# Keeping one operand sum of the wd stage in DRAM between two products

## The chip, the cores and the metric

The kernel runs on one core of one Trainium2 chip. The metric is device time in microseconds of one execution. Five engines work side by side, each with its own queue of instructions: TensorE (PE, its weight loads PEld) multiplies, VectorE (DVE) and ScalarE (ACT) do elementwise work, GpSimd (POOL) does nothing here, SyncE (SP) issues nearly all transfers. They wait for each other only where an instruction needs another's result or a buffer that another still uses.

## The reference, cut to what matters

```python
def _A_ref(x, dft_seq_re, dft_seq_im, dft_hid_re, dft_hid_im):
    a = jnp.einsum("bsd,ed->bse", x, dft_hid_re)
    b = jnp.einsum("bsd,ed->bse", x, dft_hid_im)
    return jnp.einsum("ts,bse->bte", dft_seq_re, a) - jnp.einsum("ts,bse->bte", dft_seq_im, b)
...
def _B_ref(x, w1, b1, w2):
    h = jnp.einsum("bsd,df->bsf", x, w1) + b1
    sp = jnp.log1p(jnp.exp(-jnp.abs(h))) + jnp.where(h > 0, h, jnp.zeros_like(h))
    act = h * jnp.tanh(sp)
    return jnp.einsum("bsf,fd->bsd", act, w2)
...
x = A_x
g = _sigmoid((x * gate_w).sum(-1, keepdims=True))
return g * _A_ref(x, ...) + (1 - g) * _B_ref(x, B_w1, B_b1, B_w2)
```

x has 2048 rows and 640 columns, the hidden width of the second branch is 1728, and everything is float32.

## The kernel before, in words

**Arithmetic.** A float32 matrix product is made of three products of a reduced type: each operand is split into a high part and a low part, and high x high, high x low and low x high are added up in PSUM (mm3, line 100). A split (line 91) is one ScalarE copy for the high part and one VectorE subtraction for the low one. A moving operand is a tile of 128 x 512; its two parts lie in one of nine pairs R (rh, rl), to which four pairs of W are lent later. Stationary blocks of 128 x 128 lie in 26 pairs W (wh, wl).

On top of that stands the scheme of Winograd's form of Strassen: a product of 2 x 2 blocks takes seven block products instead of eight, at the price of sums of operands and results.

**Stages.** The kernel forms u = x times the two sequence matrices (stage "seq", four problems), then y = u times the hidden matrices wd (stage "hid", two problems), then the dense layer with mish (steps in narrow pieces), then the product with w2 (stage "out", two problems). u, y and the activations go through DRAM. In each Winograd problem the moving operand has four blocks per k: a11 and a12 (columns t1), a21 and a22 (columns t2); t1 and t2 are two of the four column groups of 512. A problem has three parts, each a list of steps, one step per product and k:

- first() (line 335): the product with a11, and the column of d that isn't part of the 2 x 2 scheme.
- second() (line 376): the products "22", "21", "s2", "s1". Its sums() (line 381) loads a22, a21, a11 and forms s1 = a21 + a22 and s2 = s1 - a11. s2, the fourth product counting first()'s, is split and multiplied, and its tile goes back to the free list.
- third() (line 487): the products "12", "s3", "s4". Its sums() (line 491) loads a12, a11, a21, a22 and forms s3 = a11 - a21, then a22 - s3, which is s2 again, then s4 = a12 - s2. s4 is the operand of the last product.

In the stage of wd there are five k (kh = KD = 5), so second() has 20 steps and third() 15 per problem; in_turn (line 320) gives their order. The two problems follow each other: first() of both, then second() and third() of the first, then of the second.

**Order of the work.** Nothing is ordered by the hardware alone: a planner in the kernel's text, the loop from line 1203, writes out each engine's queue step by step. At step i it issues loads of operands for steps up to LEAD + AHEAD = 7 + 9 ahead, as long as the free list FS of 22 tiles of 128 x 512 keeps a few in reserve (spare, line 1197); it writes the preparation (sums and splits, "preps") of the step 7 ahead; then step i's matmuls; then the stores that are due; then post work and side jobs. A store is registered by store() (line 128) with a lag in steps, and its tile goes back to FS when the store has been issued. A load may not be issued before its source's store has been: `unwritten` holds the tiles that are still to be stored.

**Side jobs** are the preparation of stationary operands, for the current and the coming stages (low and top, quad_job line 644, w1_job line 661, w1c, w1r), and the gating of y. The planner keeps an account, clock["dve"], of the time that it has given to VectorE, and starts or goes on with a job only while that account is below clock["pe"] plus a limit: SLACK = -1 in the stage of wd, SLACK_D = +1 in most of the dense stage. Each tt() (line 84) adds 0.14 + 0.54 x columns/512 to it. A job also needs free tiles of W, FX (four of 128 x 640) and FS. In a few steps around the start of the dense stage ("quiet") no job runs.

The lines that the change touches or the prediction speaks of: the account at line 85, the split at 91 and 250, the matmul at 98, the loads at 147, 152 and 1214, the stores at 1223.

Of the kernel before, what the change touches and what calls it, by code (L numbers as in the profile page):

```python
# [7 lines left out]
F32 = mybir.dt.float32  # L8
F32R = mybir.dt.float32r
AF = mybir.ActivationFunctionType  # L10
OP = mybir.AluOpType

S, D, F = 2048, 640, 1728
P = 128
N = 512
# [12 lines left out]
SLACK, SLACK_UP, SLACK_D, QUIET = -1.0, 2.5, 1.0, 2  # L28
NR, NFS, NFX, NW, NL = 9, 22, 4, 26, 4
MM = 0.2267  # L30
BACK, NB = 16, 3
NLOAD = 6
QUIET_M, D_END = -1, 24
# [21 lines left out]
def fnet_mish_gate(ctx: ExitStack, tc: tile.TileContext, xn, xt, c_re, c_im, wd_re, wd_im,  # L55
# [4 lines left out]
    dr = ctx.enter_context(tc.tile_pool(name="dr", bufs=1, space=bass.MemoryType.DRAM))  # L60
# [4 lines left out]
    FS = Slots([sb.tile([P, N], F32, name=f"f{i}") for i in range(NFS)])  # L65
# [18 lines left out]
    def tt(o, a, b, op):  # L84
        clock["dve"] += 0.14 + 0.54 * a.shape[-1] / N
        nc.vector.tensor_tensor(o, a, b, op=op)  # L86
# [41 lines left out]
    def store(dst, v, f, lag=3):  # L128
        stores.append((dst, v, f, clock["step"] + (lag if clock["step"] < len(steps) - 8 else 0)))
# [117 lines left out]
                                2 + (k % KD == 0) + ((st.kind, k) not in tops), 1, 1))  # L247
            tops.add((st.kind, k))

    def c_split(key, f):  # L250
        r = OPS[key] = R.get()
        split(r[0], r[1], f)
        FS.put(f)

    def op_done(key):
        R.put(OPS.pop(key))
# [63 lines left out]
    def in_turn(kh, begin, between, end):  # L320
# [2 lines left out]
        order += [(p, k) for k in range(2, kh - 2) for p in between]  # L323
        return order + [(p, k) for p in end for k in (kh - 2, kh - 1)]

    class Problem:


        def __init__(self, st, tp, moving, finish, end=False, aside=None):
            self.st, self.moving, self.finish, self.end, self.aside = st, moving, finish, end, aside  # L330
            self.t1, self.t2 = 2 * tp, 2 * tp + 1
            self.out, self.early = st.kind == "out" and not tp, st.kind == "out" and tp


        def first(self, new=False, ks=None):
# [40 lines left out]
        def second(self):  # L376
            st, kh, t1, t2 = self.st, self.st.kh, self.t1, self.t2
            n = len(steps)
            own = {}
# [64 lines left out]
            for p, k in in_turn(kh, ("22", "21", "s2", "s1"), ("22", "21", "s2", "s1"), ("22", "21", "s2", "s1")):  # L444
                i, key = len(steps), ("c", st.kind, len(steps))
                raw, preps = [], []
                if p == "22":
                    raw = [(("a", a, i), self.moving(t, kk)) for a, t, kk in
                           ((22, t2, k + kh), (21, t2, k), (11, t1, k))]
                    preps.append(lambda k=k, raw=raw: (need((st.kind, "low", k)), sums(k, raw)))  # L450

                def mms(p=p, k=k, key=key):
                    for name, b in uses[p](k):
                        product(name, b, key, k == 0 and (p, name) in opens and not (st.kind == "out" and name != "b"),
                                k == kh - 1)
                    op_done(key)
                    if self.end and (p, k) in ends:
                        W.put(st.XA[k])
                        if k == kh - 1:
                            W.put(*[w for w in st.XT2 if w])  # L460
                preps.append(lambda p=p, k=k, key=key: c_split(key, own.pop((p, k))))
                step(raw, preps, mms, lambda p=p, k=k: post(p, k))
                if k == kh - 1:
                    takes[i] = (p == "21" or p == "s1" and 2) if self.early else 1 if p == "21" else 2
                    if self.early and p != "s1":
                        takes[i - 4] = 2
                        if p == "21":
                            self.y_load(i - 4, t2, 4)
                        else:
                            self.y_load(i - 4, *{"22": (t2, 0, 1), "s2": (t1, 2, 3)}[p])  # L470
                if (p, k) == ("21", kh - 1):
                    done = i
# [14 lines left out]
        def third(self, over=False):  # L487
            st, kh, t1, t2 = self.st, self.st.kh, self.t1, self.t2
            own = {}

            def sums(k, raws):
                a12, a11, a21, a22 = (RAW.pop(r[0]) for r in raws)
                tt(a11, a11, a21, OP.subtract)
                FS.put(a21)
                tt(a22, a22, a11, OP.subtract)
                tt(a22, a12, a22, OP.subtract)
                own.update({("12", k): a12, ("s3", k): a11, ("s4", k): a22})

            uses = {
                "12": lambda k: [("c", blocks(st.XB[k], P, 2)), ("d1", blocks(st.XB[k], 0, 1))],  # L500
                "s3": lambda k: [("a", blocks(st.XT13[k], 2 * P, 2))],
                "s4": lambda k: [("b", blocks(st.XB[k], 3 * P, 2))],
            }

            def b_out():
                f, g, (p0, p1) = FS.get(), FS.get(), PS["b"]
                copy(f, p0)
                self.finish(2, t1, f)
                copy(g, p1)
                nc.scalar.dma_start(out[3 * P:4 * P, t1 * N:(t1 + 1) * N], g)  # L510

            def post(p, k):
                if k < kh - 1:
                    return
                if self.early and p == "s4":
                    b_out()
                elif p == "s3":
                    fs = KEEP.pop("p4") + KEEP.pop("p5")
                    for ps, o in zip(PS["a"] * 2, fs):
                        tt(o, ps, o, OP.add)  # L520
                    free_banks("a")
                    for d, o in enumerate(fs):
                        if self.out:
                            at(clock["step"] + d // 2 + 1, lambda d=d, o=o: self.give(d, t2, o))
                        else:
                            self.give(d, t2, o)
                elif p == "12":
                    self.done("c", 0, t1)
                    self.done("d1", 4, t1)
                else:  # L530
                    self.done("b", 2, t1)

            for p, k in in_turn(kh, ("12", "s3", "s4"), ("12", "s3", "s4"), ("s3", "12", "s4")):
                i, key = len(steps), ("c", st.kind, len(steps))
                if self.early and p == "s4" and k >= kh - 2:
                    key = p, k
                raw, preps = [], []
                if (p, k) in {("12", k) for k in range(kh - 2)} | {("s3", kh - 2), ("s3", kh - 1)}:
                    raw = [(("a", a, i), self.moving(t, kk)) for a, t, kk in
                           ((12, t1, k + kh), (11, t1, k), (21, t2, k), (22, t2, k + kh))]  # L540
                    preps.append(lambda k=k, raw=raw: sums(k, raw))

                def by_bank(k=k):
                    j = k - (kh - 2)
                    for kk in (kh - 2, kh - 1):
                        mm3(PS["b"][j], *uses["s4"](kk)[0][1][j], *OPS["s4", kk], False, kk == kh - 1)

                def mms(p=p, k=k, key=key):
                    if self.early and p == "s4" and k >= kh - 2:
                        return by_bank(k)  # L550
                    for name, b in uses[p](k):
                        product(name, b, key, False, k == kh - 1)
                    op_done(key)
                    if self.end and p == "s4":
                        W.put(st.XB[k], st.XT13[k])
                preps.append(lambda p=p, k=k, key=key: c_split(key, own.pop((p, k))))
                step(raw, preps, mms, lambda p=p, k=k: post(p, k))
                if k == kh - 1 and p != "s3":
                    takes[i] = 3 if p == "12" else 2
                if self.out and k == kh - 1:  # L560
                    self.y_load(i - (4 if p == "s3" else 2), *{"s3": (t2, 0, 1, 2, 3), "12": (t1, 0, 1, 4), "s4": (t1, 2, 3)}[p])
                    if p == "s4":
                        at(i, lambda: FS.put(QT.pop(t1), QT.pop(t2)))
                if st.kind == "out" and (p, k) == ("s4", 1):
                    rest(t1, [("c", 0, False), ("c", 1, False), ("d1", 4, False), ("b", 2, False), ("b", 3, False)])
# [481 lines left out]
    unwritten = {id(d) for row in usc + asc + qout for d in row} | {id(d) for d in XD.values()}  # L1047
# [64 lines left out]
    hid = Stage("hid", KD, lambda k: (wd_re, wd_im)[k // KD][k % KD], neg=True)  # L1112
# [7 lines left out]
    hd = [Problem(hid, tp, lambda t, k: usc[k][t], put_y, tp == 1, aside("ph") if tp else None) for tp in range(2)]  # L1120
    ou = [Problem(fin, tp, lambda t, k: asc[k][t], put_out, False, aside("po") if tp else None) for tp in range(2)]

    stage_jobs(seq, [("low", k) for k in range(KH)])
    for k in range(KS):
        jobs.append(Job(("gate", k), simple(lambda f, k=k: gate_rows(k, f)), lambda k=k: [x_rows(k)], fx=1 + (not k)))
# [172 lines left out]
```

## Time and profile before

| what | value |
|---|---|
| median of 3 runs | 861.6 us (861.38 to 861.71) |
| the profiled execution | 862.33 us |
| its span, first to last instruction | 860.5 us |
| matmuls | 3766 |
| read from HBM, written | 180.13 MB, 52.18 MB |

| stretch of the profiled span | what runs |
|---|---|
| 0 to 397 us | stage seq |
| 397 to 519 us | stage of wd |
| 519 to 687 us | dense stage |
| 687 to 857 us | stage of w2 |

The bounds of the stages come from counting the matmuls of each stage in the code. In a row of the profile's groups "L86 DVE TENSOR_TENSOR f<-f,f ... x50 | 34.5, 689 | 1.0" means line 86 of the kernel, VectorE, output tile and inputs, 50 instructions, 34.5 us busy, 689 ns each, 1.0 us idle before them. A row of a timeline begins with the start and the duration in us. A row of stretches gives, after the stretch and its length, the busy us and the number of instructions of PE, PEld, DVE, ACT and POOL, then the granted clock, the DMA engines' mean share and GB/s. Rows of waits give the engine that waited, for whom, us in total, times and the longest. Rows of transfers give their number, KB each and the median us from issue to landing.

### The profile page before, as it was taken

How to read it: one execution, taken by the hardware profiler on the slowest of the kernel's cores; microseconds unless marked ns; L12 is line 12 of the kernel's file. 1: busy time of each engine (PE TensorE's matmuls, PEld its weight loads, DVE VectorE, ACT ScalarE, POOL GpSimd, SP SyncE). 2: the span in 40 equal slices, each digit the busy share in tenths (PEclk: the TensorE clock that was granted, in tenths of full speed). 3: DMA queues.
4: the chain of work that ended last, by engine and by line, in shares of the span. 5: the costliest groups of instructions: out<-in, count | busy, mean ns of one | idle time of the engine just before them, and what ended most of it. 6: DMA issues, size and time to landing. Idle time of an engine off the chain costs nothing.

```text
span 860.5 us, 12305 instructions
## 1 busy us (share of the span) xinstructions
PE 856.2 (100%) x3766; PEld 708.4 (82%) x3766; DVE 732.6 (85%) x1281; ACT 485.6 (56%) x903; POOL 0.2 (0%) x4
## 2 busy tenths in 40 slices
PE   9999999999999999999999999999999999999998
PEld 8888888888888888888888888888888888888886
DVE  6999988889879789998998897886578979898993
ACT  6756646464555545657656657764646756542442
POOL 0000000000000000000000000000000000000000
PEclk9999999999999999999999999999999999999999
DMA  9975758885768899898676968879998789485952
GB/s 348 345 255 198 252 164 309 281 287 198 255 234 287 280 343 363 274 316 287 207 261 242 319 197 309 287 231 370 357 377 308 230 283 315 152 289 178 353 185 110
DMA packets 126978, 233.15 MB, mean 271 GB/s; under 512 B 14656, under 2 KB 17216, under 8 KB 126912
## 3 DMA queue, kind: packets, MB, share of 16 engines
q1 hardware_dynamic: 126480, 231.72, 77.9%
q8 instruction: 29, 0.48, 0.2%
q10 hardware_dynamic: 432, 0.66, 0.2%
q14 instruction: 37, 0.30, 0.1%
HBM read 180.13 MB, written 52.18 MB: 270 GB/s over the span
## 4 chain that ended last, share of the span: by engine, by line
PE 100%; ACT 0%; issue 0%
PE ps L98 100%; ACT f L89 0%
## 5 line engine op out<-in xcount | busy, mean ns | idle before, releaser
L98 PE MATMUL ps<-rh,wh 128*128 128x512 f32 (+1 forms) x1062 | 412.1, 389 | 0.0
L98 PE MATMUL ps<-rh,wl 128*128 128x512 f32 x1046 | 405.9, 389 | 0.0
L98 PE MATMUL ps<-rl,wh 128*128 128x512 f32 x1045 | 405.9, 389 | 0.0
L89 ACT ACTIVATE rh<-f 128x512 fp32r<-128x512 f32 x419 | 250.8, 626 | 182.7 <-DVE f L86 101.7
L86 DVE TENSOR_TENSOR rl<-f,rh 128x512 fp32r<-128x512 f32 x417 | 272.5, 686 | 41.3 <-ACT rh L89 40.1
L98 PEld LDWEIGHTS ps<-rh,wh 128*128 128x128 f32 x1062 | 199.5, 188 | 41.6 <-DVE f L86 0.3
L98 PEld LDWEIGHTS ps<-rl,wh 128*128 128x128 f32 x1045 | 196.6, 188 | 40.9
L98 PEld LDWEIGHTS ps<-rh,wl 128*128 128x128 f32 x1046 | 196.3, 188 | 40.7
L86 DVE TENSOR_TENSOR f<-f,f 128x512 f32<-128x512 f32 x305 | 208.4, 688 | 9.6 <-DMA f<-act 2.2
L89 ACT ACTIVATE f<-ps 128x512 f32<-128x512 f32 (+1 forms) x145 | 83.2, 596 | 75.2 <-PE ps L98 66.7
L89 ACT ACTIVATE wh<-f 128x512 fp32r<-128x512 f32 (+3 forms) x173 | 76.7, 484 | 46.7 <-DVE f L86 36.5
L86 DVE TENSOR_TENSOR wl<-f,wh 128x512 fp32r<-128x512 f32 (+3 forms) x172 | 82.3, 512 | 20.5 <-ACT wh L89 20.4
L86 DVE TENSOR_TENSOR f<-ps,f 128x512 f32<-128x512 f32 x100 | 65.5, 683 | 16.9 <-PE ps L98 16.7
L98 PE MATMUL ps<-wh,wh 128*128 128x512 f32 x205 | 79.8, 389 | 0.0
L98 PE MATMUL ps<-wl,wh 128*128 128x512 f32 x200 | 77.8, 389 | 0.0
L98 PE MATMUL ps<-wh,wl 128*128 128x512 f32 x199 | 77.4, 389 | 0.0
L98 PEld LDWEIGHTS ps<-wh,wh 128*128 128x128 f32 x205 | 38.5, 188 | 8.2 <-ACT f L89 0.2
L98 PEld LDWEIGHTS ps<-wl,wh 128*128 128x128 f32 x200 | 37.5, 188 | 7.8
L98 PEld LDWEIGHTS ps<-wh,wl 128*128 128x128 f32 x199 | 37.4, 188 | 7.7
L732 ACT ACTIVATE f<-f,b1s 128x512 f32<-128x512 f32 x36 | 25.5, 721 | 31.5 <-DVE f L86 31.5
L86 DVE TENSOR_TENSOR wl<-fx,wh 128x640 fp32r<-128x640 f32 (+3 forms) x50 | 33.7, 680 | 5.9 <-ACT wh L89 5.9
L89 ACT ACTIVATE wh<-fx 128x640 fp32r<-128x640 f32 (+4 forms) x51 | 31.1, 615 | 5.9 <-DMA fx<-in_xn_dram 3.5
(36 smaller groups left out, 176.5 us busy)
## 6 DMA issues: line engine op xcount, KB each, us to landing
f<-in_c_re_dram SPq DMA_DIRECT2D x128, 256.0 KB, 4.0
f<-in_c_im_dram SPq DMA_DIRECT2D x128, 256.0 KB, 4.5
f<-act SPq DMA_DIRECT2D x87, 256.0 KB, 4.9
f<-u SPq DMA_DIRECT2D x80, 256.0 KB, 5.0
act<-f SPq DMA_DIRECT2D x54, 256.0 KB, 5.1
f<-in_xt_dram SPq DMA_DIRECT2D x49, 256.0 KB, 4.6
u<-f SPq DMA_DIRECT2D x40, 256.0 KB, 3.1
y<-f SPq DMA_DIRECT2D x40, 256.0 KB, 4.9
```

The lines of the kernel that those rows point to most:

```text
L86: nc.vector.tensor_tensor(o, a, b, op=op)
L89: nc.scalar.activation(o, a, AF.Copy, scale=scale)
L98: nc.tensor.matmul(ps, a, b, start=start, stop=stop, skip_group_check=True)
L732: nc.scalar.activation(o[rows], src[rows], AF.Mish, bias=b1s[rows, f:f + 1])
```

## The change

Each problem of the stage of wd (S2_OF names "hid" alone) gets five tiles in DRAM, s2[k]. When the s2 of a k has been split in second(), its tile isn't given back at once but stored there, with a lag of one step (S2_LAG). third()'s sums() loads s2[k] in the place of a22 and leaves out the subtraction that forms it again. The new tiles are added to `unwritten`. The other stages stay as they are.

```diff
+S2_LAG, S2_OF = 1, ("hid",)
...
-    def c_split(key, f):
+    def c_split(key, f, dst=None):
         r = OPS[key] = R.get()
         split(r[0], r[1], f)
-        FS.put(f)
+        if dst is None:
+            FS.put(f)
+        else:
+            store(dst, f, f, S2_LAG)
...
+            n = len(problems)
+            problems.append(self)
+            self.s2 = [dr.tile([P, N], F32, name=f"s2_{n}_{k}") for k in range(st.kh)] if st.kind in S2_OF else []
...
-                preps.append(lambda p=p, k=k, key=key: c_split(key, own.pop((p, k))))
+                preps.append(lambda p=p, k=k, key=key: c_split(key, own.pop((p, k)), self.s2[k] if p == "s2" and self.s2 else None))
...
-                tt(a22, a22, a11, OP.subtract)
+                if not self.s2:
+                    tt(a22, a22, a11, OP.subtract)
                 tt(a22, a12, a22, OP.subtract)
...
+                    if self.s2:
+                        raw[-1] = ("s2", i), self.s2[k]
                     preps.append(lambda k=k, raw=raw: sums(k, raw))
...
+    unwritten.update(id(d) for p in problems for d in p.s2)
```

More of the change, by code (lines that the diff above doesn't have):

```diff
@@ L324, in in_turn @@
         return order + [(p, k) for p in end for k in (kh - 2, kh - 1)]
+    problems = []
     class Problem:
```

## The prediction

> **What bounds the kernel now.** I begin with the shares of the engines and the chain that ended last, because a change that takes work from VectorE pays only where VectorE, or something that waits for it, sets the end.
>
> ```profile
> span 860.5 us, 12305 instructions
> ...
> PE 856.2 (100%) x3766; PEld 708.4 (82%) x3766; DVE 732.6 (85%) x1281; ACT 485.6 (56%) x903; POOL 0.2 (0%) x4
> ```
> ```profile
> 0.77 856.26 PE ps L98 x3766
> 857.03 0.02 issue
> 857.05 0.60 ACT f L89
> ```
>
> Of the page's rows the second gives TensorE's matmul track 100% and VectorE 85%. The other three are the chain in order of time: from 0.77 us on, 856.26 us are one unbroken piece of matmuls, and only the last copy and store of the output stand behind it. VectorE is not in the chain.
>
> A busy matmul track could still run slowly, so I look at its rate, by stretches of 100 us, and then at all the waits of TensorE and of its weight loads.
>
> ```profile
> 100.00:200.00 100.00, 100.00 (x443) 82.79 (x442) 89.10 (x151) 49.49 (x84) 0.00 (x0) 1.00 0.77 260
> ...
> 400.00:500.00 100.00, 100.00 (x443) 82.81 (x442) 91.22 (x160) 65.34 (x124) 0.00 (x0) 1.00 0.77 267
> 500.00:600.00 100.00, 100.00 (x442) 82.47 (x441) 81.99 (x161) 64.66 (x134) 0.00 (x0) 1.00 0.80 278
> ```
> ```profile
> PE ps L98 <- PEq L1286: 0.8, 1, 0.8
> ```
> ```profile
> PEld ps L98 <- issue: 0.7, 1, 0.7
> PEld ps L98 <- DVE f L86: 0.3, 1, 0.3
> PEld ps L98 <- ACT f L89: 0.2, 1, 0.2
> ```
>
> 442 or 443 matmuls start in each stretch, whatever VectorE does in it (82 to 91 us of the 100), at a granted clock of 1.00: one about every 0.227 us. TensorE waits once, for 0.8 us, before its first matmul. The weight loads wait three times, 0.7 us at the start and 0.3 and 0.2 us later; those last two are all that the other engines cost TensorE in the whole execution. So there is hardly any waiting that a lighter VectorE could give back.
>
> The Trainium skill, "Perfetto Trace Analysis", section "Identifying the Most-Contended Engine", holds that the busy share of matmuls is no good measure of the distance to the roofline and that the weight loads' share is a better one. By that rule the 82% of the weight loads would say that 18% of the time is headroom. The row of counts decides here: the rate is the same in every stretch, so whatever headroom there is lies inside a matmul's own 0.227 us, and this change leaves number and shape of the matmuls alone.
>
> **The stage of wd.** Each of its two problems has 270 matmuls (45 in first(), 120 in second(), 105 in third()), and the matmuls before it end at 397 us. Behind it stands the dense stage.
>
> ```profile
> 397.00:519.00 122.00, 122.00 (x540) 101.03 (x539) 111.44 (x196) 79.48 (x151) 0.00 (x0) 1.00 0.75 259
> 519.00:580.00 61.00, 61.00 (x270) 50.17 (x269) 49.52 (x105) 43.60 (x94) 0.00 (x0) 1.00 0.78 268
> ```
> ```profile
> L86 DVE TENSOR_TENSOR f<-f,f 128x512 f32<-128x512 f32 x50 | 34.5, 689 | 1.0
> ```
>
> In the stage's 122 us VectorE is busy for 111.4. Of that, 50 sums of two operands take 34.5 us; 50 is what the code makes it, two per k in second() and three in third(), five k, two problems.
>
> **What is removed.** One sum per k in third(): 10 instructions of 689 ns, 6.9 us of VectorE. It comes off an engine that TensorE does not wait for in these 122 us: 0 us of the time. The next rows show how far ahead VectorE's results are; the first writes the low part of an operand, the second is the first matmul that streams it.
>
> ```profile
> 441.31 0.68 DVE L86 TENSOR_TENSOR wl<-f,wh 128x512 fp32r<-128x512 f32 x1
> ```
> ```profile
> 447.04 0.39 PE L98 MATMUL ps<-wl,wh 128*128 128x512 f32 x1
> ```
>
> Ready at 441.99, used at 447.04: 5.0 us of lead, the shortest between 430 and 460 us when I pair all operands with their matmuls in this way. The lead may grow by up to 3.4 us per problem. That has no value by itself.
>
> **What is added.** Ten stores of 256 KB, and ten loads of s2 in the place of ten loads of u, so the number of loads stays.
>
> ```profile
> f<-u SPq DMA_DIRECT2D x80, 256.0 KB, 5.0
> act<-f SPq DMA_DIRECT2D x54, 256.0 KB, 5.1
> ...
> u<-f SPq DMA_DIRECT2D x40, 256.0 KB, 3.1
> ```
> ```profile
> L1223 SPq DMA_DIRECT2D u<-f x40: 319/382/1286, 94.3 to 401.8; - x40
> ```
>
> - Issue: 10 x 382 ns = 3.8 us of SyncE's queue over 122 us. Hidden: loads are issued up to LEAD + AHEAD = 16 steps before their step, and a step here is 225 / 35 = 6.4 matmuls, 1.46 us.
> - Traffic: 2.6 MB more in a stage that moves 259 GB/s, about 10 us at its mean rate or 0.083 of its volume; the engines' share rises from 0.75 to some 0.81. Hidden while the loads keep their lead.
> - The store's own wait: it needs the sum, which VectorE formed before it split 22, 21 and s2 of that k. On SyncE the store comes one step after the split of s2 was planned. At most it waits about 1 us, and the loads of u and of weights queued behind it have some 20 us of lead.
> - The reload's wait for its store to land. Counting out the planner's loops, there are at least six steps between the two for every k, 6 x 1.46 = 8.8 us (some 6 us where SyncE runs in bursts), against a landing after 3.1 (u) to 5.1 us (act). No wait, or a small one.
> - A slot of FS is held for one to three steps longer, and its next load waits for the store's reading instead of for the split. There are 22; the planner then takes a load one or two steps later, out of 16.
>
> No row of before shows this reload. From above it is bounded by store and load in sequence for each k, 10 x (3.1 + 5.0) = 81 us if nothing hid any of it; from below by zero, or by the 0.5 us of the weight loads' later waits if the lighter VectorE removed them. I take zero, because loads of u with the same size, queue and lead delay no matmul.
>
> The Trainium skill, "DMA: Bandwidth & Descriptors", section "Anatomy of one DMA — SWDGE (gpsimd) path", puts most of a fixed 2 us into the receipt of the write, worst for HBM, and its section "Two DMAs through the same engine are not ordered" asks for a wait on the first transfer before a reader is issued. By its fit an estimate for 256 KB is 2.6 us each way; the trace's 3.1 and 5.0 us are longer, and the sum stays zero by both as long as the six steps stand between.
>
> **What is moved.** The planner counts each sum as 0.14 + 0.54 = 0.68 us of VectorE and starts side work when that account is 1 us behind TensorE's. Five sums fewer lower it by 3.4 us per problem, so it draws forward what comes next: the weights of the dense stage.
>
> ```profile
> 449.34 0.90 SPq L147 DMA_DIRECT2D fx<-in_w1a_dram  x2
> ...
> 469.01 1.65 SPq L147 DMA_DIRECT2D fx<-in_w1a_dram  x2
> ...
> 482.25 0.81 SPq L147 DMA_DIRECT2D fx<-in_w1a_dram  x2
> ...
> 511.20 0.80 SPq L147 DMA_DIRECT2D fx<-in_w1a_dram  x2
> ...
> 532.75 3.28 SPq L147 DMA_DIRECT2D fx<-in_w1a_dram  x2
> ```
>
> The pair at 449.34 is issued when the job before it has given its rows back. In the new account that job can start some ten steps sooner, so this load should come at 436 to 442 us. Jobs that need three free pairs of W stay where third() frees them; later, from 511 us on, about one job of w1 (some 4 us of VectorE) gets done before the dense stage instead of in it. In that stage the cover is thin:
>
> ```profile
> 562.42 0.69 DVE L86 TENSOR_TENSOR rl<-f,rh 128x512 fp32r<-128x512 f32 x1
> ...
> 563.60 0.39 PE L98 MATMUL ps<-rl,wh 128*128 128x512 f32 x1
> ```
> ```profile
> 573.21 0.43 DVE L86 TENSOR_TENSOR f<-fx,f 128x256 f32<-128x256 f32 x1
> ...
> 573.55 0.68 DVE L86 TENSOR_TENSOR f<-ps,f 128x512 f32<-128x512 f32 x1
> ...
> 574.29 0.19 PEld L98 LDWEIGHTS ps<-rh,wh 128*128 128x128 f32 x1 [0.30 <-DVE f L86]
> ```
>
> Ready at 563.11, used at 563.60: 0.49 us. And at 574.29 the weight load waited for an add that reads a bank of PSUM and stood behind the preparation of weights; the wait of 0.30 us is the row seen above. If the jobs come earlier, such places get better by up to the 0.5 us; if another piece falls in front of such an add, they get worse.
>
> **Sum**, against the profiled execution: 862.33 = span 860.5 + 1.83 around it. Sums removed 0, stores and loads 0, moved work between -0.5 and some tenths, I take -0.1. That execution lies 0.7 above the median of the runs, 861.6; taken off the median, the forecast is **861.5 us**.
>
> **Rivals.**
> - *A new stall in the dense stage; slower.* The same weights, in another order, can put a burst in front of an add for which TensorE waits. One burst is four sums of 0.42 us (the row at 573.21 is the last of one), 1.7 us, and there are three pairs of fp: 1.7 us if it strikes once, 863.2, and 5.1 if in each, 866.6. It decides from the point where VectorE is more than 0.49 us later than now at such a place. For it: the 0.49 and the 0.30 us. Against it: VectorE is busy for 49.5 of 61 us there and gets less to do, and the planner holds its account to the same limit. From about 590 us on the planner's account of before runs at its floor (3 us behind TensorE), so both schedules meet again.
> - *The reload takes the place of the sum; slower.* If store and load follow each other closely, SyncE stands 5 us for each k, and everything behind it too. It decides when the delay exceeds the lead of the loads, some 20 us: four waits in a row. One problem's five would then cost 5 x 5 - 20 = 5 us, 866.6. Against it: six steps lie between.
> - *VectorE's time counts after all; faster.* All 6.9 us off: 854.7. Against it: the counts by stretches and the list of waits. Half of it would already be past the bound.
> - *The change doesn't do what it says.* If u were still read beside s2, ten more loads would show; the diff replaces the entry in the list, so nothing of this is left but a count to check.
>
> **How the numbers follow.** About 0.2% (1.7 us) is what a measurement of this kernel can tell from no change. The forecast's own case, 861.0 to 862.5, has 0.85; the stall in the dense stage 0.10, the reload 0.02, VectorE's gain 0.03. Within 0.2% thus 0.85, slower 0.12, faster 0.03. The range goes from 861.0 (both later waits gone, and the runs' own spread of 0.3 us below) to 863.2 (one burst).
>
> **What would show it.** Right: TensorE's matmuls again one piece of about 856 us, 3766 of them; f<-f,f in the stage 40 instead of 50, VectorE some 7 us less busy in all; u read 70 times, ten stores to s2 and ten loads; the first weight load after w1b near 440 us instead of 449.34. Wrong: a wait of TensorE or its weight loads of over 0.5 us between 519 and 580 us (first rival), SyncE waiting for s2 to land with operands late behind it (second), fewer than 850 us of matmuls (third).

## The result and the profile after

The changed kernel takes 862.89 us (median of 22 runs, 862.69 to 863.96), the kernel before 861.77 us (22 runs, 861.38 to 862.62). The ratio is 1.0013, 95% interval 1.0007 to 1.0019: slower by 1.1 us. The time is inside the forecast range and within the 0.2%, but its sign is the wrong one: the forecast took 0.1 us off the kernel before, and the interval of the ratio lies wholly on the slower side.

What was to be seen of the change itself is there. These are rows of the page of the changed kernel, one of its groups in the stretch from 397 to 519 us, and three of its transfers (the program's name of the new tiles, numbers left out, is s). All lines have moved down: 87 is the old 86, 90 the old 89, 99 the old 98.

```profile
span 860.9 us, 12296 instructions
...
PE 855.9 (99%) x3766; PEld 707.5 (82%) x3766; DVE 725.4 (84%) x1271; ACT 485.8 (56%) x903; POOL 0.2 (0%) x4
```
```profile
L87 DVE TENSOR_TENSOR f<-f,f 128x512 f32<-128x512 f32 x40 | 26.6, 686 | 0.3
```
```profile
f<-u SPq DMA_DIRECT2D x70, 256.0 KB, 4.8
...
s<-f SPq DMA_DIRECT2D x10, 256.0 KB, 5.4
f<-s SPq DMA_DIRECT2D x10, 256.0 KB, 5.0
```

Ten sums fewer, 7.2 us of VectorE less over the whole execution (732.6 to 725.4), ten loads of u replaced, ten stores added. The time did not come from there. Next the two stretches, and all waits of the weight loads:

```profile
397.00:519.00 122.00, 122.00 (x540) 101.03 (x539) 106.95 (x194) 80.10 (x156) 0.00 (x0) 1.00 0.80 278
519.00:580.00 61.00, 60.37 (x265) 49.14 (x264) 48.50 (x101) 43.34 (x93) 0.00 (x0) 1.00 0.85 293
```
```profile
PEld ps L99 <- ACT f L90: 0.9, 1, 0.9
PEld ps L99 <- DVE f L87: 0.8, 2, 0.6
PEld ps L99 <- issue: 0.7, 1, 0.7
PEld ps L99 <- ACT wh L90: 0.2, 1, 0.2
```

In the stage of wd 540 matmuls start, as before: nothing lost, nothing won. In the 61 us behind it 265 start instead of 270. The waits of 0.2 and 0.3 us of before have grown to 0.9 and 0.8.

To add them up I took the starts of all matmuls from the 21st on, and counted what an interval above 0.229 us exceeds 0.2267 us by. Before: 0.22 us in all, 0.05 us of it around 560 us and 0.17 us from 574 us on. After: 1.37 us, at the same two places, 0.76 us around 559 us (the expectations below write 0.75) and 0.61 us from 573.9 us on. The 1.15 us between the sums is the 1.1 us of the runs. The profiled spans differ by 0.4 us only (860.5 and 860.9), because the first 20 matmuls took 6.77 us in the one profile and 5.89 us in the other. That start differs from profile to profile, though all eleven kernels profiled here begin alike. When it is taken off each span together with the waits, 853.55 to 853.86 us are left in all eleven: start and waits account for the spans to 0.3 us.

The chain that ended last was one piece of matmuls before. Now it breaks in the dense stage (start, us, what):

```profile
0.77 557.77 PE ps L99 x2454
558.54 0.06 issue
558.60 0.02 ACTq L90
558.61 0.13 issue
558.74 0.40 ACT wh L90
559.14 1.46 ACT f L90 x3
...
573.75 0.61 DVE f L87
574.36 0.04 issue
574.40 282.90 PE ps L99 x1246
```

From 558.5 to 574.4 us it runs through ScalarE and VectorE, and behind 574.4 all is matmuls again. So this is the prediction's first rival, in the stretch that it named, and with the sign that it gave for it, a wait of over 0.5 us between 519 and 580 us.

### The profile page after: what moved, and what is told of

The parts are those of the page before. It is cut to its first block, busy times and chain, and to the rows that moved or that the text cites. A ratio compares the mean times of both kernels' runs of the same rounds, so it can differ in the third digit from the quotient of the medians.

```text
span 860.9 us, 12296 instructions
## 1 busy us (share of the span) xinstructions
PE 855.9 (99%) x3766; PEld 707.5 (82%) x3766; DVE 725.4 (84%) x1271; ACT 485.8 (56%) x903; POOL 0.2 (0%) x4
## 4 chain that ended last, share of the span: by engine, by line
PE 98%; DVE 1%; ACT 1%; issue 0%; DVEq 0%; ACTq 0%
PE ps L99 98%; DVE f L87 0%; DVE wl L87 0%; ACT wh L90 0%; ACT f L90 0%; ACT f L744 0%; DVE fx L87 0%; DVE rl L87 0%; ACT rh L90 0%; DVEq L87 0%; ACTq L90 0%
## 5 line engine op out<-in xcount | busy, mean ns | idle before, releaser
L87 DVE TENSOR_TENSOR f<-f,f 128x512 f32<-128x512 f32 x295 | 200.5, 688 | 9.7 <-DMA f<-act 2.7
```

## The experiments

Theory 1: with ten sums fewer in its account the planner starts the side jobs of the dense stage in other steps, and this new order makes TensorE wait. Its rival: the ten stores and reloads, with their traffic and the tiles that they hold, delay something. A third possibility is that VectorE's time in the stage of wd matters in itself. Counted out from the planner's loops, the jobs w1 1 to w1 5 begin at steps 340, 349, 352, 357 and 362 before, and at 329, 340, 349, 354 and 358 in the changed kernel; the steps of the stage end at 335. Counted in the same way, all pieces of all jobs keep the steps of before in the first, the third and the fourth experiment, and those of the changed kernel in the second. All ratios are to the kernel before on the same chip.

### The change in the old order

```diff
                 if not self.s2:
                     tt(a22, a22, a11, OP.subtract)
+                else:
+                    clock["dve"] += 0.14 + 0.54
```

> The change as it is, but the planner's account still adds the 0.68 us of each sum that is left out, so the side jobs run in the order of before. Theory 1 (the new order of the weight jobs in the dense stage is what costs): the time of before, 861.8 us (ratio 0.999 to 1.001), and TensorE's waits between 519 and 580 us back from 1.37 to at most 0.4 us. Rival (the ten stores and reloads cost): the time of the change, 862.9 us, ratio 1.0013, with the waits of over 1 us still there. That VectorE's 6.9 us count: 855 us.

Measured: 861.79 us against 862.17, ratio 0.9997 (0.9988 to 1.0006); TensorE's waits 0.25 us. Sums gone, stores and reloads there, and the time is that of before. The stores and reloads cost nothing that can be seen, and the order of the jobs is all that is left.

### The old arithmetic in the new order

```diff
                 tt(a22, a22, a11, OP.subtract)
+                if st.kind == "hid":
+                    clock["dve"] -= 0.14 + 0.54
```

> The kernel before, its sum formed twice as ever and nothing stored, but the account does not count the ten sums, so the side jobs run in the order of the changed kernel. Theory 1: slower as the change is, 862.9 us or a little more, since VectorE still has the ten sums to do (ratio 1.0008 to 1.003), with waits of 1 to 2.5 us between 519 and 580 us. Rival (stores and reloads cost): 861.8 us, waits 0.2 to 0.4 us.

Measured: 863.43 us against 862.17, ratio 1.0013 (1.0004 to 1.0022), the ratio of the change; waits 1.38 us.

```profile
PEld ps L98 <- ACT f L89: 0.9, 1, 0.9
PEld ps L98 <- DVE f L86: 0.8, 2, 0.6
PEld ps L98 <- issue: 0.7, 1, 0.7
PEld ps L98 <- ACT wh L89: 0.5, 1, 0.5
```

The two rows that count are those of the changed kernel to the tenth. Nothing is stored here and no sum is saved: the new order alone makes the loss.

### The stores alone

```diff
-                if not self.s2:
-                    tt(a22, a22, a11, OP.subtract)
+                tt(a22, a22, a11, OP.subtract)
...
-                    if self.s2:
-                        raw[-1] = ("s2", i), self.s2[k]
```

> s2 is stored as in the change, but third() loads u and forms the sum again; the stored copy is not read. Order of the side jobs as before. Theory 1: 861.8 us (0.999 to 1.001), waits at most 0.4 us. Rival (the stores, their traffic and the tiles held longer cost): some or all of the 1.1 us, 862.3 to 862.9 us.

Measured: 861.88 us against 862.17, ratio 0.9998 (0.9989 to 1.0007); waits 0.23 us. No cost.

### One more sum

```diff
                 tt(a22, a22, a11, OP.subtract)
+                if st.kind == "hid":
+                    nc.vector.tensor_tensor(a21, a12, a22, op=OP.subtract)
                 tt(a22, a12, a22, OP.subtract)
```

a21 goes back to the free list behind these lines instead of ahead of them.

> The kernel before with one more sum for each k in third() of the stage of wd, into a tile that is no longer needed, and not counted in the account: 10 x 0.69 = 6.9 us more of VectorE, the order of everything else as before. Theory 1 with the prediction's first step (VectorE's time in this stage lies beside the matmuls): 861.8 us, 0.999 to 1.001. Rival (VectorE's time in this stage reaches the end, and the dense stage starts later on VectorE): up to 6.9 us more, 868.7, or 0.5 to 2 us if only the rest of it is carried into the dense stage.

Measured: 861.87 us against 862.17, ratio 0.9997 (0.9988 to 1.0006); waits 0.27 us.

```profile
397.00:519.00 122.00, 122.00 (x540) 101.02 (x539) 115.78 (x202) 77.56 (x147) 0.00 (x0) 1.00 0.75 253
```

VectorE is busy for 115.8 of the 122 us, 4.3 more than before in this stretch (and 1.7 more in the next 61 us), and 540 matmuls start as ever. Ten sums of 0.69 us are worth nothing here, added or taken away.

### Where the order bites: one step more before the splits

The first wait in the changed kernel, by its timeline (start, us, engine, what; the bracket gives idle time and what ended it), between the three adds that free banks and the matmul that waits:

```profile
553.72 1.87 DVE L87 TENSOR_TENSOR f<-ps,f 128x512 f32<-128x512 f32 x3
555.51 0.41 DVE L87 TENSOR_TENSOR wl<-fx,wh 128x256 fp32r<-128x256 f32 x1
555.85 0.48 DVE L87 TENSOR_TENSOR wl<-f,wh 128x128 fp32r<-128x128 f32 x2
556.25 0.55 DVE L87 TENSOR_TENSOR wl<-fx,wh 128x384 fp32r<-128x384 f32 x1
556.72 0.41 DVE L87 TENSOR_TENSOR fx<-fx,fx 128x256 f32<-128x256 f32 x1
```
```profile
557.96 0.42 DVE L87 TENSOR_TENSOR f<-fx,f 128x256 f32<-128x256 f32 x1
...
558.42 0.42 ACT L90 ACTIVATE wh<-f 128x256 fp32r<-128x256 f32 x1 [0.61 <-DVE f L87]
...
558.74 0.40 ACT L90 ACTIVATE wh<-fx 128x256 fp32r<-128x256 f32 x1
...
559.05 1.55 ACT L90 ACTIVATE f<-ps 128x512 f32<-128x512 f32 x3
...
559.68 0.19 PEld L99 LDWEIGHTS ps<-wh,wh 128*128 128x128 f32 x1 [0.90 <-ACT f L90]
```

Read it backwards. The weight load at 559.68 waits for the first of three copies out of PSUM (559.05). That copy stands in ScalarE's queue behind two splits of a w1 job (558.42, 558.74), and the first of these waited 0.61 us for the last of the job's four sums on VectorE (557.96). Ahead of the sums VectorE has the last piece of one job (555.51, 555.85) and the first piece of the next (556.25) in a row. In the kernel before, only a first piece stands there:

```profile
554.59 1.87 DVE L86 TENSOR_TENSOR f<-ps,f 128x512 f32<-128x512 f32 x3
556.39 0.54 DVE L86 TENSOR_TENSOR wl<-fx,wh 128x384 fp32r<-128x384 f32 x1
556.86 0.41 DVE L86 TENSOR_TENSOR fx<-fx,fx 128x256 f32<-128x256 f32 x1
```
```profile
559.19 1.57 ACT L89 ACTIVATE f<-ps 128x512 f32<-128x512 f32 x3
```

From the end of the adds to the copy: 559.19 - 556.46 = 2.7 us before, 559.05 - 555.59 = 3.5 us after. The 0.7 us between them are the extra piece (555.51 to 556.25), and nearly all of the wait of 0.76 us. In all of this VectorE's total did not grow: it is busy for 48.5 us of this stretch instead of 49.5.

If that is so, the copy need not wait for any less work, only for its place in the queue to be free (theory 1a). To test it, each w1 job rests two steps instead of one between its sums and its splits:

```diff
         tt(t[:, B2], ga[:, B2], t[:, A2], OP.subtract)
-        yield 1
+        yield 2
```

> The changed kernel, but each w1 job rests two steps instead of one between its four sums and the splits that read them. Theory 1a (ScalarE's queue stands at a split that needs a sum just formed, and the copy that frees a bank stands behind it): the waits of TensorE between 519 and 580 us fall from 1.37 to at most 0.5 us, time 861.8. Theory 1b (VectorE simply has too much to do there): the same work in nearly the same place, waits of 1 us or more, 862.9.

Measured: 862.14 us against 861.91, ratio 0.9999 (0.9991 to 1.0008); waits 0.11 us, less than the kernel before has. ScalarE's queue at the same place:

```profile
557.78 2.05 ACT L90 ACTIVATE f<-ps 128x512 f32<-128x512 f32 x4
559.68 0.44 ACT L90 ACTIVATE wh<-f 128x256 fp32r<-128x256 f32 x1
```

Four copies, the three among them, now run through ahead of the split. But the longer rest also moves the jobs' steps, w1 2 begins at 349 again, and the double piece is no longer there. So this run supports theory 1a and does not tell it from the double piece; the last experiment does.

The Trainium skill, "Perfetto Trace Analysis", section "Optimization Strategy", says that a gap that repeats on the engine that should be saturated can mean too little SBUF or PSUM. The waits here are waits for PSUM banks, and by that rule one would look for more PSUM; with the eight banks that the kernel has, another order of the queues took the waits from 1.37 to 0.11 us.

### The old order and the longer rest

The edits of the first experiment and of this one together.

> The order of before (the ten sums left out but still counted), and the rest of two steps as well. Theory 1a: the waits of before, 0.22 us, go too; 861.6 us, at most 0.3 us below the kernel before, ratio 0.9995 to 1.0. Theory 1b: 861.8 us, waits 0.2 to 0.4.

Measured: 861.97 us against 861.91, ratio 1.0001 (0.9992 to 1.0010); waits 0.10 us. The waits of before are halved, and 0.1 us can't be seen in the time. Nothing more is left to win here: all the waits of the kernel before were worth 0.2 us.

### The double piece split up

```diff
-elif loaded and loaded[0][2] + (5 if i in narrow else 3) <= i and len(W.free) >= loaded[0][0].w:
+elif loaded and i != nm - 1 and loaded[0][2] + (5 if i in narrow else 3) <= i and len(W.free) >= loaded[0][0].w:
```

> The changed kernel, but in the one step where the last piece of a w1 job and the first piece of the next are written in a row (the first step after the pause in which no job runs), the next job starts a step later. All other jobs start as in the changed kernel. Theory 1 in detail (that double piece is what comes in front of the copy that frees the bank at 558.8 us): the first wait falls from 0.75 to at most 0.3 us, the second near 574 us stays at 0.3 to 0.6; time 862.1 to 862.5. If the double piece has no part in it, both stay and the time is 862.9.

Measured: 863.65 us against 861.91, ratio 1.0018 (1.0009 to 1.0026). The first wait is gone, as expected. The second is 1.41 us instead of 0.3 to 0.6, and the sum 1.70 us: a miss in the total.

```profile
554.43 1.87 DVE L87 TENSOR_TENSOR f<-ps,f 128x512 f32<-128x512 f32 x3
```
```profile
574.24 0.56 DVE L87 TENSOR_TENSOR wl<-fx,wh 128x384 fp32r<-128x384 f32 x1 [1.21 <-ACT wh L90]
...
574.72 0.68 DVE L87 TENSOR_TENSOR f<-ps,f 128x512 f32<-128x512 f32 x1
...
575.45 0.19 PEld L99 LDWEIGHTS ps<-rh,wh 128*128 128x128 f32 x1 [1.67 <-DVE f L87]
```

Here the roles are exchanged: the add that frees the bank (574.72) stands on VectorE behind a low part (574.24) that waited 1.21 us for ScalarE. In the changed kernel the add at this place is this one:

```profile
573.66 0.68 DVE L87 TENSOR_TENSOR f<-ps,f 128x512 f32<-128x512 f32 x1
```

The two traces can't be laid on each other by the clock, since their first 20 matmuls differ by 0.7 us (5.89 and 6.61); so I count from the three adds, at 553.72 in the changed kernel and at 554.43 here. The later add follows after 19.94 us there and after 20.29 us here: VectorE comes to it 0.35 us later. TensorE, which no longer lost its 0.76 us at the first place, comes to it that much sooner. Together these are the 1.1 us by which the second wait grew (0.61 to 1.70 us, with what follows it). My expectation took the two waits as separate; what TensorE doesn't lose at the first place it loses at the second, because VectorE is late there all the same.

By the planner's loops all four pieces of the shifted job move by a step, its sums and splits too, and no other job moves. So this run takes away the double piece and gives the copies more room at once, and doesn't show the part of the double piece alone.

### A lower limit in the dense stage

```diff
-SLACK, SLACK_UP, SLACK_D, QUIET = -1.0, 2.5, 1.0, 2
+SLACK, SLACK_UP, SLACK_D, QUIET = -1.0, 2.5, 0.0, 2
```

> The changed kernel with the limit of the account in the dense stage at 0 instead of +1 us. The jobs up to the first wait keep their steps, those after it come later by up to a step. Theory 1: the first wait stays at 0.75 us, the second changes. If the waits hang on VectorE's total in the stage alone: both change together.

Measured in a single run: 863.15 us; waits 0.82 us, the first at 0.77, as in the changed kernel, and the second down to 0.05. One run can't place the time within some tenths, so the trace has to tell. Between 519 and 580 us VectorE is busy for 49.1 us, no less than the 48.5 of the changed kernel. Each wait goes with the steps of the jobs just ahead of it, and not with VectorE's load in the stage.

### One job alone rests longer

```diff
         tt(t[:, B2], ga[:, B2], t[:, A2], OP.subtract)
-        yield 1
+        yield 2 if f == 3 else 1
```

> The changed kernel, with the rest of two steps between sums and splits for one w1 job alone, the one whose splits stand ahead of the first late copy. The double piece ahead of its sums stays where it is, and all jobs begin in the steps of the changed kernel; only this job's last two pieces are written a step later. Theory 1a (the place of the copy in ScalarE's queue): the first wait falls from 0.75 to at most 0.1 us though the double piece is still there. If the double piece itself is what delays the copy: 0.75 stays. The second wait, near 574 us, may grow to as much as 1.4, as it did when a job was shifted by a step; the time would then be 862.5 to 863.5 us.

Measured: 862.60 us against 862.15, ratio 1.0004 (0.9995 to 1.0013), so the time doesn't settle it; the trace does. The waits are 0.66 us, all of them from 574 us on; the first wait is gone.

```profile
556.75 0.48 DVE L87 TENSOR_TENSOR wl<-f,wh 128x128 fp32r<-128x128 f32 x2
557.15 0.55 DVE L87 TENSOR_TENSOR wl<-fx,wh 128x384 fp32r<-128x384 f32 x1
```
```profile
558.12 2.05 ACT L90 ACTIVATE f<-ps 128x512 f32<-128x512 f32 x4
560.03 0.45 ACT L90 ACTIVATE wh<-f 128x256 fp32r<-128x256 f32 x1
```

The double piece is there, last of one job and first of the next, and the copies run through ahead of the split all the same. So both have a part in the first wait: the double piece delays the sum, and the split that waits for it holds the copy. Without the split in front of the copy the wait is gone (this run). With the split in front, but without the extra piece, it is 0.05 us: that is the kernel before, where at this place a first piece, the sums and the splits of a job stand in the same three steps, 349 to 351. The second wait grew less than I allowed for, from 0.61 to 0.66 us: counted from the three adds, VectorE comes to its add 0.68 us sooner than in the changed kernel (573.88 - 554.62 = 19.26 us), nearly as much as TensorE does. Why it comes sooner here and later in the run of the double piece wasn't taken apart any further.

### All runs beside each other

| kernel | waits in the trace, us | median less that of before on the same chip, us |
|---|---|---|
| before | 0.22 | |
| changed | 1.37 | 1.12 |
| change, old order | 0.25 | -0.38 |
| old arithmetic, new order | 1.38 | 1.26 |
| stores alone | 0.23 | -0.29 |
| one more sum | 0.27 | -0.30 |
| longer rest | 0.11 | 0.23 |
| old order, longer rest | 0.10 | 0.06 |
| double piece split up | 1.70 | 1.74 |
| lower limit (one run) | 0.82 | 1.24 |
| one job rests longer | 0.66 | 0.45 |

## Why the prediction was right and where it was wrong

- **What bounds the kernel**: right. In all eleven kernels the time follows TensorE's own waits, within the half microsecond or so that the medians scatter, and the profiled spans follow them to 0.3 us once the first 20 matmuls are taken off. The rate was not quite the same in every stretch, though: the first 100 us hold 428 matmuls, since the first 20 are slower.
- **Sums removed, 0 us**: right, by the run that adds ten more and by the first experiment.
- **Stores and reloads, 0 us**: right, by the first and the third experiment. Two readings in it were off, without effect. The landing took 5.4 us, above the 3.1 to 5.1 that I bounded it by, and between store and reload the planner's loops put five to eight steps, not at least six. No reload had to wait for its store all the same; the closest was issued 1.06 us after its store had landed. SyncE did wait for the stores to land, three times, 4.3 us in all, the longest 2.1 us (the row of its waits reads "SPq L1228 <- DMA s<-f: 4.3, 3, 2.1"). But the run that stores and never reloads has these waits too, 5.0 us in four. The two long ones in the changed kernel, 2.1 and 1.9 us, end at loads of u (434.46 and 489.81) into the very tile that the store was reading: the tile that is held longer, and not the reload. The lead of the loads covered them.
- **What is moved: the step that failed.** That the jobs come earlier was right, and nearly so by how much: the first pair of weights came at 434.9 us instead of 449.3 (forecast 436 to 442), and w1 one job earlier. But the sum's term was "between -0.5 and some tenths, I take -0.1", with the reason that "if the jobs come earlier, such places get better". It measured +1.15 us in the waits and +1.12 us in the time. An earlier job is not a better place: what mattered was which pieces stood in a row between the freeing of a bank and its next use. For that I looked at the wrong margin. I paired operands with matmuls and found 0.49 us at 563.60; that lead grew to 0.89 us in the changed kernel, just as I argued. The thin places were the banks of PSUM. At 559.84 us the weight load of the kernel before already waited 0.2 us for a copy, that is, it had no margin at all, and I counted this row as something to gain.
- **The first rival** had place and sign, and of the mechanism the main part, that another piece falls in front of the work that frees a bank; its chance was 0.10. What fell in front at the first place was not the burst of four sums, which stands there in the kernel before too, but the last piece of another job, 0.74 us of VectorE, and the bank was freed by a copy on ScalarE and not by an add. So the price was not 1.7 us for one burst: two smaller delays made 1.15 us together. The threshold at the first place was not 0.49 us but zero. For the second place the runs show that the wait goes with the order of the jobs; which piece makes it in the changed kernel stays open.
- **The range** held by luck. Its upper end, 863.2, was one burst of 1.7 us, which is not what happened.

## What to carry to other kernels

Where one engine is saturated and the others are ordered by a plan, a change of a cost in that plan is a change of the whole later order; price the order, not the instructions taken out. A wait of 0.2 us on the saturated engine is a place without margin, not a small gain, and whatever delays the work that ends this wait counts in full (here 0.74 us of VectorE made 0.71 us more of waiting). A copy that frees a bank should not be queued behind an instruction that waits for another engine.

## What the runs showed of the hardware that was not expected

The first 20 matmuls took between 5.86 and 6.86 us in the profiles of these kernels, with the same program there. At first their starts lie 0.427 us apart and later 0.227 us, and the turn comes at different times: in the changed kernel the last interval of 0.427 us is the eighth, in the kernel before the fifteenth (the 0.213 us between are matmuls of half the width), while the granted clock reads 1.00 in both. That spread of 1.0 us is as large as the effect under study, so spans of single profiles could not have settled it, while the summed waits agreed to about 0.01 us between the kernel that stores s2 (1.37) and the one that only has its order (1.38).
